# First pair of an FFT-then-SoLU kernel: its loads of x in 128 rows, the small tables elsewhere in the queue, the weight conversions in another order

## The chip, the cores and the metric

The kernel runs on one core of a Trainium2 chip. A core has five engines that run their own instruction streams and wait for each other on semaphores: TensorE (PE, matrix products; PEld is its weight load), VectorE (DVE), ScalarE (ACT), GpSimd (POOL) and SyncE (SP), which only issues transfers. Sixteen DMA engines move the data between the chip's memory (HBM) and the on-chip memory (SBUF, 128 partitions). Transfers issued by SP stand in one queue (q1 in the profile), those issued by POOL in another (q0). The metric is the device time of one execution in microseconds (us), lower is better. A profiled execution also gives a span, from the first to the last instruction, a little less than its time.

## The reference, cut to what matters

A two-dimensional Fourier transform of which the real part is kept, then a token-wise two-layer network with a softmax-weighted activation and a normalization:

```python
batch, seq, dim = (8, 3136, 256)
X = np.fft.fft(x, axis=1)
X = np.fft.fft(X, axis=2)
x = X.real.astype(np.float32).reshape(B * S, D)      # 25088 tokens of 256
h = x @ w_in                                         # w_in: 256 x 1024
h_max = np.max(h, axis=-1, keepdims=True)
e = np.exp(h - h_max)
sm = e / (np.sum(e, axis=-1, keepdims=True) + 1e-09)
solu = h * sm
mu = np.mean(solu, axis=-1, keepdims=True)
var = np.mean((solu - mu) ** 2, axis=-1, keepdims=True)
ln = (solu - mu) / np.sqrt(var + 1e-06) * g_ln       # g_ln: 1024
return (ln @ w_out).astype(np.float32)               # w_out: 1024 x 256
```

x and g_ln are 32-bit floats; w_in and w_out arrive as 64-bit floats, which the kernel itself turns into 32-bit ones ("conversions" below).

## The kernel before

The sequence of 3136 is taken as 49 x 64. The batch of 8 is worked in 4 *pairs* of two samples; a pair has 2 x 49 = 98 rows (`PR`), so a tile of x has 98 partitions. For a pair, x comes in 8 *pieces* c = 0 to 7 (`NC`), each of 4 positions x 256 features: `load` (L118) fetches a tile `xa` through SP and, by a gather with row indices from `idx`, the mirrored positions `xb` through POOL. One such transfer is 98 rows of 4 KB. For the first pair, pieces 2 to 5 stand in borrowed buffers (`room`, two of them, each for two pieces), pieces 0, 1 and later 6, 7 in the two `xa` and `xb` buffers, so that pieces 6 and 7 can only be fetched once pieces 0 and 1 are folded.

Per piece DVE adds the mirror (`add_mirror`, L137) and folds the features (`fold`, L153) into `y` (two buffers); PE applies the first transform (`transform1`, L185: eight matmul records a piece, into four PSUM banks in turn), ACT copies the two results to `z` (L218), and SP writes part of them to DRAM (`keep`, L223). Once all eight pieces are there, `turn` (L225) reads them back in another layout as `g`, `transform2` makes the 256 features of a *unit* (one k1 of a pair, 100 units), and the steady loop over units follows: up-projection (L279), softmax, blocks of transposes, down-projection, store.

Besides the first pair's pieces the opening prepares the weights. w_in is loaded in four raw pieces of 512 KB (L581). Each is converted by DVE and ACT: `exponent_in(i)` is one DVE instruction (L584) and three ACT instructions, the confinement (L608, L610, L612); `narrow_in(i)` is four DVE instructions (L584, L625, L628, L634), of which L628 needs the confined exponents. Then PE multiplies the converted w_in by the feature transform Q (`product_in`, L685), and ACT keeps the product as `Wi` (L689). `mid` (L676) makes a small operand from Q on ACT. w_out comes in two transfers of 1 MB into the buffer of pieces 2 and 3 (L700), is converted in the same manner by `exponent_out` and `narrow_out`, scaled by `g_ln`, and summed by `mean_out` (L730). `scale_out` (L704) scales g_ln. `load_tables` (L662) fetches Q (257 KB) and g_ln; F (`f_tab`, 230 KB) is transform 1's table.

The order of the opening is written out by hand (lines 784 to 861, under `manual_schedule`): each engine runs its instructions in the order in which this program text calls them. That holds for the queues too. The opening's transfers on SP are, in order: idx, w_in pieces 0 and 1, xa 0, F, w_in 2, xa 1, w_in 3, xa 2, xa 3, Q, g_ln, xa 4, xa 5, and then, as buffers come free, xa 6, zd of piece 0, xa 7, a row x0, zd of pieces 1 and 2, w_out, the first table T. A DMA that SP issues may first wait for an earlier one, as eight semaphores are used in turn. POOL issues the gathers of pieces 0 to 7 in order. On DVE the conversions 0 and 1 precede piece 0, exponent 2 comes ahead of piece 0, conversion 2 and exponent 3 ahead of piece 1, conversion 3 ahead of piece 2. The lines that fetch g_ln:

```python
662        def load_tables(self):
663            self.Q = fpool.tile([P, KD, D + 1], FP32, tag="ev", name="Q", bufs=1)
664            nc.sync.dma_start(out=self.Q, in_=q_tab.rearrange("(c p) d -> p c d", p=P))
665            nc.sync.dma_start(out=g_ln, in_=moe_g_ln.rearrange("(c p) -> p c", p=P))
```

g_ln thus arrives as 128 partitions of 8 single numbers.

Of the kernel before, what the change touches and what calls it, by code (L numbers as in the profile page):

```python
# [9 lines left out]
FP32 = mybir.dt.float32  # L10
# [7 lines left out]
P = 128  # L18


N1, N2 = 49, 64
NK = N1 // 2 + 1
NH = N2 // 2
PR = 2 * N1
ZR = 4 * NK
CH = 4
NC = NH // CH
# [11 lines left out]
def shared(b, n):  # L39

    return WHOLE // 2 <= b < n - 1 and all(u % NK for u in (2 * b, 2 * b + 1))
# [3 lines left out]
def kernel(  # L45
# [19 lines left out]
    nc = tc.nc  # L65
    B, S, D = x.shape
    FF = moe_w_in.shape[1]
    KF = FF // P
# [4 lines left out]
    x_g = x.rearrange("b (n1 g l) d -> (b n1 g) (l d)", n1=N1, l=CH)  # L73
    x_pn = x.rearrange("b (n1 n2) d -> (b n1) n2 d", n2=N2)
# [3 lines left out]
    xpool = ctx.enter_context(tc.tile_pool(name="xpool", bufs=2))  # L78
# [6 lines left out]
    fpool = ctx.enter_context(tc.tile_pool(name="fpool", bufs=2))  # L85
# [3 lines left out]
    F = const.tile([PR, 6, ZR], FP32, name="F")  # L89
# [6 lines left out]
    ident = const.tile([P, P], FP32, name="ident")  # L96
    neg_half = const.tile([P, 2], FP32, name="neg_half")
    idx = const.tile([P, NP * (NC + NK)], I32, name="idx")
    w_mid = const.tile([P, FF], FP32, name="w_mid")
    g_ln = const.tile([P, KF], FP32, name="g_ln")  # L100
# [17 lines left out]
    def load(pr, c, room=None):  # L118

        r = slice(pr.p * PR, (pr.p + 1) * PR)  # L120
        if room is None:
            xa = xpool.tile([PR, CH, D], FP32, tag="xa", name="xa")
            xb = xpool.tile([PR, CH, D], FP32, tag="xb", name="xb")
        else:
            xa, xb = (t.rearrange("p (l d) -> p l d", d=D) for t in room)
        nc.sync.dma_start(out=xa, in_=x_pn[r, c * CH + 1 : (c + 1) * CH + 1, :])
        i = pr.p * NC + c
        nc.gpsimd.indirect_dma_start(
            out=xb.rearrange("p l d -> p (l d)"), out_offset=None, in_=x_g,
            in_offset=bass.IndirectOffsetOnAxis(ap=idx[0:PR, i : i + 1], axis=0))  # L130
        x0 = None
        if c == NC - 1:
            x0 = xpool.tile([PR, 1, D], FP32, tag="x0", name="x0", bufs=1)
            nc.sync.dma_start(out=x0, in_=x_pn[r, 0:1, :])
        pr.raw[c] = (xa, xb, x0)

    def add_mirror(pr, c, engine, part=None):  # L137

        xa, xb, _ = pr.raw[c]
        rows = (0, CH) if part is None else (part * CH // 2, (part + 1) * CH // 2)  # L140
        r = slice(rows[0], min(rows[1], CH - 1 if c == NC - 1 else CH))
        a, rb = xa[:, r, :], xb[:, ::-1, :][:, r, :]
        i = engine.tensor_tensor(out=a[:, :, 1:D], in0=a[:, :, 1:D], in1=rb[:, :, D - 1 : 0 : -1], op=ALU.add)
        if part is None:
            engine.tensor_tensor(out=a[:, :, 0:1], in0=a[:, :, 0:1], in1=rb[:, :, 0:1], op=ALU.add)
        return i
# [6 lines left out]
    def fold(pr, c):  # L153

        xa, _, x0 = pr.raw.pop(c)
        pr.y[c] = xpool.tile([PR, CH, D], FP32, tag="y", name="y")
        sides = [(pr.y[c], xa)]
        if c == NC - 1:
            pr.y0 = xpool.tile([PR, 1, D], FP32, tag="y0", name="y0", bufs=1)
            sides.append((pr.y0, x0))  # L160
        for o, i in sides:
            fold_features(o, i)
            nc.vector.tensor_copy(out=o[:, :, 0:129:128], in_=i[:, :, 0:129:128])  # L163
# [473 lines left out]
    class Weights:  # L637
# [24 lines left out]
        def load_tables(self):  # L662
            self.Q = fpool.tile([P, KD, D + 1], FP32, tag="ev", name="Q", bufs=1)
            nc.sync.dma_start(out=self.Q, in_=q_tab.rearrange("(c p) d -> p c d", p=P))
            nc.sync.dma_start(out=g_ln, in_=moe_g_ln.rearrange("(c p) -> p c", p=P))

        def load_table(self, i):
            k1 = slice(KG, NK) if i else slice(0, KG)
# [32 lines left out]
                                  in_=moe_w_out.bitcast(I32).rearrange("(c p) f -> p c f", p=P)[:, c])  # L701

        def scale_out(self):
            nc.scalar.mul(out=g_ln, in_=g_ln, mul=2.0 ** -20)  # L704

        def exponent_out(self, i):
            self.units.append(exponent(moe_w_out, self.raw[:, 2 * i * NW : 2 * (i + 1) * NW]))
# [76 lines left out]
    with tc.manual_schedule():  # L784
        pairs = [Pair(p) for p in range(NP)]
        first, weights = pairs[0], Weights()
# [3 lines left out]
        rooms = {}  # L790
        for c in range(2, 6, 2):
            room = fpool.tile([P, 2, KF, 4, 64], FP32, tag="uT", name="room", bufs=2)
            room = room[0:PR].rearrange("p w c i m -> p (w c i m)").rearrange("p (a n) -> p a n", a=4)
            rooms[c], rooms[c + 1] = [room[:, i] for i in (0, 1)], [room[:, i] for i in (2, 3)]
        weights.load_in()
        for c in range(4):
            weights.piece_in(c)
            if c:
                load(first, c - 1, rooms.get(c - 1))
            if c == 1:  # L800
                nc.sync.dma_start(out=F, in_=f_tab)
        load(first, 3, rooms[3])
        weights.load_tables()
        for c in range(4, 6):
            load(first, c, rooms[c])
        nc.vector.memset(ones, 1.0)
        nc.vector.memset(neg_half, -0.5)
        bits(top_bit, neg_half[:, 0:1].bitcast(I32), 31, ALU.logical_shift_right, 31, ALU.logical_shift_left)
# [6 lines left out]
        for c in range(NC):  # L815

            if c == 0:
                weights.narrow_in(0)
                weights.narrow_in(1)
            elif c < 3:  # L820
                weights.narrow_in(c + 1)
            if c < 2:
                weights.exponent_in(c + 2)
            add_mirror(first, c, nc.vector)
            fold(first, c)
            if c == NC - 1:
                for i in range(2):
                    weights.exponent_out(i)
                confine(weights.units[0], True)
                weights.narrow_out(0)  # L830
            if c + 6 < NC:
                load(first, c + 6)
            if c == 3:
                weights.place_out()
                for i in range(2):
                    weights.load_out(i)
                weights.load_table(0)
                weights.mid()
                weights.scale_out()
            for s in range(CH // 2):  # L840
                if c == NC - 1:
                    confine(weights.units[0], parts=(s,))
                transform1(first, c * CH // 2 + s)
            if c == 3:
                weights.keep_in(0, weights.product_in(0))
            elif c == 4:
                odd = weights.product_in(1, (0,))
            elif c == 5:
                weights.product_in(1, (1,), odd)
# [136 lines left out]
        for i in range(whole + 1, len(units) + lag + 1):  # L986
# [84 lines left out]
            if i in (len(units), len(units) + 1):  # L1071
                w = i - len(units)
# [7 lines left out]
def _tables(B, S, D):  # L1080

    import numpy as np

    def cs(num, den):
        a = 2.0 * math.pi * (num % den) / den
        return np.cos(a), np.sin(a)

    n1, k1 = np.arange(N1)[:, None], np.arange(NK)[None, :]
    c, s = cs(n1 * k1, N1)
    cm, sm = cs((n1 - N1 // 2) * k1, N1)  # L1090
    zero = np.zeros_like(c)
    tabs = [(c, s), (s, -c), (c, zero), (s, zero), (zero, cm), (zero, sm)]
    f = np.zeros((2, N1, 6, NK, 2, 2))
    for t, (u, v) in enumerate(tabs):
        for b in range(2):
            f[b, :, t, :, b, 0], f[b, :, t, :, b, 1] = u, v
    k = (np.arange(NK)[:, None] + N1 * np.arange(N2)[None, :])[None]
    n2 = (np.arange(NH) + 1) % NH
    c, s = cs(n2[:, None, None] * k, S)
    t = np.stack([c, -s])  # L1100
    t[1, -1] = 1.0 - 2.0 * (k[0] % 2)
    m, d = np.arange(D)[:, None], np.arange(D)[None, :]
    q = np.where(d <= D // 2, cs(m * d, D)[0], -cs(m * (d - D // 2), D)[1])

    q = np.concatenate([q, q[:, D // 2 : D // 2 + 1]], axis=1)
    q[:, D // 2] = 0.0
    sign = np.where(np.arange(P) == 0, 1.0, -1.0)[:, None]
    row = np.arange(B)[:, None] * N1 + np.arange(N1)[::-1]

    load = row.reshape(-1, PR, 1) * (N2 // CH) + N2 // CH - 1 - np.arange(NC)  # L1110
    mirror = np.zeros((P, B // 2 * (NC + NK)), np.int32)
    mirror[:PR, : B // 2 * NC] = load.transpose(1, 0, 2).reshape(PR, -1)
    rows = np.arange(B)[:, None, None] * S + (N1 - np.arange(NK)) + N1 * np.arange(N2)[::-1, None]
    rows = rows.reshape(B // 2, P, NK).transpose(1, 0, 2).reshape(P, -1)
    for b in range(rows.shape[1] // 2):
        if shared(b, rows.shape[1] // 2):

            two = rows[:, 2 * b : 2 * b + 2].reshape(2, 2, 32, 2).transpose(1, 0, 3, 2)
            rows[:, 2 * b : 2 * b + 2] = two.reshape(2, P).T
    mirror[:, B // 2 * NC :] = rows  # L1120
    return {
        "f_tab": f.reshape(PR, 6, ZR).astype(np.float32),
        "t_tab": t.reshape(2 * NH, NK, N2).astype(np.float32),
        "q_tab": q.astype(np.float32),
        "sign": sign.astype(np.float32),
        "mirror": mirror,
    }
# [32 lines left out]
```

## Time and profile before

| what | us |
|---|---|
| median of 3 runs (lowest, highest) | 1126.72 (1125.56, 1128.06) |
| the profiled execution | 1127.41 |
| its span | 1125.6 |
| first matmul of piece 0 | 18.80 |
| first matmul of piece 1 | 26.64 |
| first matmul of pieces 2 and 3 | 31.71 |
| first weight product on PE | 37.96 |
| w_out's first conversion on DVE | 47.66 |
| first matmul of transform 2 | 57.36 |

The rows below the span are starts in the timeline of the profiled execution, counted from the span's start. In the profile a line such as `L143` is a line of the kernel's text; a name such as `y<-xa` tells what an instruction writes and reads; `xN` counts instructions that were merged into one row. Idle time in brackets is that of the engine just before the row, with the engine and instruction, or the transfer, that ended it. PE's granted clock over the span is 0.999 of full speed.

### The profile page before, as it was taken

The numbers are of one execution on the slowest core, as the hardware profiler recorded it, in microseconds if no ns is written. First come the engines' busy times: TensorE is split into PE (matmuls) and PEld (weight loads), VectorE is DVE, ScalarE is ACT, GpSimd is POOL, SyncE is SP. The second block draws the span as 40 slices with busy tenths as digits, with TensorE's granted clock in tenths as the row PEclk, the third lists the DMA queues.
The fourth block names the chain that finished last, engine by engine and source line by source line (L and its number), as shares of the span: only waits on it lengthen the run. The fifth ranks groups of instructions, "written<-read, shape, count | busy, mean of one in ns | idle before, by whom it ended". The sixth has DMA issues, their size and how long they took to land. (4 is left out here: it accounts for less than half of the span.)

```text
span 1125.6 us, 22002 instructions
## 1 busy us (share of the span) xinstructions
PE 1093.1 (97%) x7030; PEld 874.1 (78%) x7030; DVE 980.5 (87%) x1440; ACT 798.2 (71%) x1946; POOL 807.5 (72%) x707
## 2 busy tenths in 40 slices
PE   1999999999999999999999999999999999999998
PEld 1556888787787787878877787878877788778888
DVE  6899889888889888898888988898988899888984
ACT  3578777777766777777767777777776777777771
POOL 3048888776887888865878788876776676766665
PEclk9999999999999999999999999999999999999999
DMA  9773798766978889766889797876786785865665
GB/s 236 211 205 82 172 188 202 175 148 152 176 174 167 194 181 187 195 146 144 158 165 183 173 192 181 200 179 143 154 154 143 141 163 125 157 144 112 142 133 126
DMA packets 458569, 185.77 MB, mean 165 GB/s; under 512 B 425774, under 2 KB 440374, under 8 KB 458456
## 3 DMA queue, kind: packets, MB, share of 16 engines
q1 hardware_dynamic: 444568, 145.96, 62.3%
q0 software_dynamic: 13888, 38.42, 13.2%
q8 instruction: 57, 0.93, 0.4%
q14 instruction: 56, 0.46, 0.1%
HBM read 44.78 MB, written 38.80 MB: 74 GB/s over the span
## 5 line engine op out<-in xcount | busy, mean ns | idle before, releaser
L279 PE MATMUL ps_h<-Wi,q 128*128 128x512 f32 x800 | 361.6, 593 | 0.5 <-DVE nmax L300 0.2
L455 POOL TENSOR_TENSOR S<-uT 128x512 f32<-128x512 f32 x186 | 237.3, 1276 | 107.1 <-DVE u L315 35.8
L462 PE MATMUL ps_m<-Ws,S 128*128 128x128 f32 x2304 | 296.0, 275 | 0.0
L462 PEld LDWEIGHTS ps_m<-Ws,S 128*128 128x128 f32 x2304 | 279.5, 192 | 3.2 <-issue 0.2
L322 ACT ACTIVATE h<-u,usum 128x1024 f32<-128x1024 f32 x196 | 225.0, 1148 | 72.3 <-DVE u L315 72.3
L279 PEld LDWEIGHTS ps_h<-Wi,q 128*128 128x128 f32 x800 | 144.2, 190 | 145.0 <-issue 141.9
L315 DVE SCALAR_TENSOR_TENSOR u<-h,u 128x1024 f32<-128x1024 f32 x196 | 233.8, 1228 | 10.9 <-ACT u L308 10.8
L308 ACT ACTIVATE u<-h,nmax 128x1024 f32<-128x1024 f32 x196 | 223.3, 1141 | 2.3 <-DVE nmax L300 1.1
L386 DVE STREAM_TRANSPOSE v<-u 128x2048 f32<-128x2048 f32 x88 | 203.4, 2311 | 3.1
L462 PE MATMUL ps_m<-Wo,uT 128*128 128x128 f32 x1536 | 203.7, 276 | 0.0
L462 PEld LDWEIGHTS ps_m<-Wo,uT 128*128 128x128 f32 x1536 | 187.9, 192 | 1.2 <-issue 1.2
L300 DVE CUSTOM_DVE_ANT_0 h<-ev,ps_h 128x1024 f32<-128x1024 f32 x100 | 122.1, 1221 | 17.1 <-DVE ev L292 9.2
L549 POOL DMA_INDIRECT out_dram<-ot,idx x96 | 111.1, 1157 | 30.0 <-issue 12.8
L300 DVE CUSTOM_DVE_ANT_0 h<-h,ps_h 128x1024 f32<-128x1024 f32 x96 | 117.2, 1221 | 14.6 <-DVE nmax L300 0.7
L455 POOL TENSOR_TENSOR S<-uT,S 128x512 f32<-128x512 f32 x93 | 118.8, 1277 | 7.2
L455 POOL TENSOR_TENSOR S<-S,uT 128x512 f32<-128x512 f32 x93 | 118.6, 1276 | 7.3
L292 DVE SCALAR_TENSOR_TENSOR ev<-w_mid,r,ps_h 128x1024 f32<-128x1024 f32 x99 | 122.8, 1241 | 0.9 <-PE ps_h L279 0.7
L462 PE MATMUL ps_m<-Ws,uT 128*128 128x128 f32 x768 | 101.8, 276 | 0.0
L462 PE MATMUL ps_m<-Wo,S 128*128 128x128 f32 x768 | 101.4, 275 | 0.0
L215 PE MATMUL ps_m<-y,F 98*100 98x258 f32 (+3 forms) x288 | 72.7, 388 | 25.9 <-DVE y L163 24.2
L243 PEld LDWEIGHTS ps_m<-T,g 128*128 128x128 f32 x400 | 60.1, 191 | 47.3 <-issue 45.7
L497 ACT ACTIVATE ot<-ps_m,rs 128x256 f32<-128x256 f32 x96 | 45.4, 473 | 70.4 <-PE ps_m L462 50.4
(109 smaller groups left out, 1232.1 us busy)
## 6 DMA issues: line engine op xcount, KB each, us to landing
uT<-v SPq DMA_DIRECT2D x752, 128.0 KB
g<-zd POOLq DMA_DIRECT2D x72, 160.0 KB, 5.0
out_dram<-ot SPq DMA_DIRECT2D x176, 64.0 KB
xa<-in_x_dram SPq DMA_DIRECT2D x28, 392.0 KB
zd<-z SPq DMA_DIRECT2D x24, 400.0 KB
raw_in<-in_moe_w_in_dram SPq DMA_DIRECT2D x4, 512.0 KB
raw_out<-in_moe_w_out_dram SPq DMA_DIRECT2D x2, 1024.0 KB
room<-in_x_dram SPq DMA_DIRECT2D x4, 392.0 KB
```

Source lines behind the costliest of these rows:

```text
L215: nc.tensor.matmul(o[..., cs], F[:, 2 * t + h, :], i[..., cs], start=first, stop=True, skip_group_check=True)
L243: nc.tensor.matmul(o, g[:, k, h * P : (h + 1) * P], table, start=(h == 0), stop=True, skip_group_check=True)
L279: nc.tensor.matmul(ps[:, fs], t.q[:, c * P : (c + 1) * P], Wi[:, c, fs], start=True, stop=not whole_even)
L292: nc.vector.scalar_tensor_tensor(out=t.ev, in0=w_mid, scalar=t.r, in1=ps, op0=ALU.mult, op1=ALU.add)
L300: nc.vector.tensor_tensor_reduce(out=t.h[s], in0=t.h[0] if s else t.ev, in1=t.odd, scale=1.0 if s else -0.5, scalar=3.0e38, op0=ALU.add, o ...
L308: nc.scalar.activation(out=t.u[s], in_=t.h[s], func=ACT.Exp, bias=t.nmax[:, s : s + 1], scale=-1.0, accum_out=t.esum[:, s : s + 1])
L315: t.last = nc.vector.scalar_tensor_tensor(out=t.u[s], in0=t.h[s], scalar=-1.0, in1=t.u[s], op0=ALU.mult, op1=ALU.mult, accum_out=t.usum[:, ...
L322: nc.scalar.activation(out=t.h[s], in_=t.u[s], func=ACT.Square, bias=t.usum[:, s : s + 1], scale=-float(FF), accum_out=t.ssq[:, s : s + 1])
L386: nc.vector.transpose(out=t.batch.v[:, :, t.w], in_=t.both.rearrange("p s (g n) -> p (s g) n", n=32))
L455: i = engine.tensor_tensor(out=S[j], in0=a, in1=b, op=op)
L462: nc.tensor.matmul(o, a[:, c], b[:, c], start=start and c == 0, stop=c == n - 1, skip_group_check=True)
L549: dma = nc.gpsimd.indirect_dma_start(out=out, out_offset=bass.IndirectOffsetOnAxis(ap=idx[:, i : i + 1], axis=0), in_=t.ot[s], in_offset=None)
```

## The change

- `load` takes 128 rows (`P`) for the first pair, both for `xa` and for the gather of `xb`; the tiles and the borrowed rooms have 128 partitions, and everything that computes reads rows 0 to 97 of them. Rows 98 to 127 are loaded and not read. The index table gets row numbers for those rows. Other pairs load 98 rows as before; the row x0 too.
- g_ln is fetched by `load_gain` as 8 rows of 128 numbers into a buffer of another tile's rotation (`ot1`), and `scale_out` turns it into 128 x 8 by a transpose on PE into a PSUM bank, from which ACT's scaling reads.
- On SP the order becomes: idx, w_in pieces 0 and 1, xa 0, F, g_ln, w_in 2, xa 1, xa 2, w_in 3, xa 3, xa 4, xa 5, Q, and then xa 6 and the rest as before.
- Exponent 2 comes between piece 0's `add_mirror` and `fold` and no longer ahead of both; conversion 2 stays ahead of piece 1; exponent 3 goes from ahead of piece 1 to between piece 2's `add_mirror` and `fold`; conversion 3 goes from ahead of piece 2 to behind its fold. The confinements on ACT move with the exponents: that of exponent 3 now follows the copies of piece 1.
- `mid` goes behind piece 3's transform; `scale_out` stays ahead of it.

```diff
--- before.py
+++ after.py
@@ -118,16 +118,18 @@
     def load(pr, c, room=None):
 
         r = slice(pr.p * PR, (pr.p + 1) * PR)
+        rows = PR if pr.p else P
         if room is None:
-            xa = xpool.tile([PR, CH, D], FP32, tag="xa", name="xa")
-            xb = xpool.tile([PR, CH, D], FP32, tag="xb", name="xb")
+            xa = xpool.tile([P, CH, D], FP32, tag="xa", name="xa")
+            xb = xpool.tile([P, CH, D], FP32, tag="xb", name="xb")
         else:
             xa, xb = (t.rearrange("p (l d) -> p l d", d=D) for t in room)
-        nc.sync.dma_start(out=xa, in_=x_pn[r, c * CH + 1 : (c + 1) * CH + 1, :])
+        nc.sync.dma_start(out=xa[0:rows], in_=x_pn[r.start : r.start + rows, c * CH + 1 : (c + 1) * CH + 1, :])
         i = pr.p * NC + c
         nc.gpsimd.indirect_dma_start(
-            out=xb.rearrange("p l d -> p (l d)"), out_offset=None, in_=x_g,
-            in_offset=bass.IndirectOffsetOnAxis(ap=idx[0:PR, i : i + 1], axis=0))
+            out=xb[0:rows].rearrange("p l d -> p (l d)"), out_offset=None, in_=x_g,
+            in_offset=bass.IndirectOffsetOnAxis(ap=idx[0:rows, i : i + 1], axis=0))
+        xa, xb = xa[0:PR], xb[0:PR]
         x0 = None
         if c == NC - 1:
             x0 = xpool.tile([PR, 1, D], FP32, tag="x0", name="x0", bufs=1)
@@ -662,7 +664,10 @@
         def load_tables(self):
             self.Q = fpool.tile([P, KD, D + 1], FP32, tag="ev", name="Q", bufs=1)
             nc.sync.dma_start(out=self.Q, in_=q_tab.rearrange("(c p) d -> p c d", p=P))
-            nc.sync.dma_start(out=g_ln, in_=moe_g_ln.rearrange("(c p) -> p c", p=P))
+
+        def load_gain(self):
+            self.gain = fpool.tile([P, D], FP32, tag="ot1", name="gain", bufs=3)[0:KF, 0:P]
+            nc.sync.dma_start(out=self.gain, in_=moe_g_ln.rearrange("(c p) -> c p", p=P))
 
         def load_table(self, i):
             k1 = slice(KG, NK) if i else slice(0, KG)
@@ -701,7 +706,9 @@
                                   in_=moe_w_out.bitcast(I32).rearrange("(c p) f -> p c f", p=P)[:, c])
 
         def scale_out(self):
-            nc.scalar.mul(out=g_ln, in_=g_ln, mul=2.0 ** -20)
+            ps = result(2)[:, 0:KF]
+            nc.tensor.matmul(ps, self.gain, ident[0:KF, 0:KF], is_transpose=True, start=True, stop=True)
+            nc.scalar.mul(out=g_ln, in_=ps, mul=2.0 ** -20)
 
         def exponent_out(self, i):
             self.units.append(exponent(moe_w_out, self.raw[:, 2 * i * NW : 2 * (i + 1) * NW]))
@@ -790,19 +797,20 @@
         rooms = {}
         for c in range(2, 6, 2):
             room = fpool.tile([P, 2, KF, 4, 64], FP32, tag="uT", name="room", bufs=2)
-            room = room[0:PR].rearrange("p w c i m -> p (w c i m)").rearrange("p (a n) -> p a n", a=4)
+            room = room.rearrange("p w c i m -> p (w c i m)").rearrange("p (a n) -> p a n", a=4)
             rooms[c], rooms[c + 1] = [room[:, i] for i in (0, 1)], [room[:, i] for i in (2, 3)]
         weights.load_in()
-        for c in range(4):
-            weights.piece_in(c)
-            if c:
-                load(first, c - 1, rooms.get(c - 1))
-            if c == 1:
-                nc.sync.dma_start(out=F, in_=f_tab)
-        load(first, 3, rooms[3])
+        weights.piece_in(0)
+        weights.piece_in(1)
+        load(first, 0)
+        nc.sync.dma_start(out=F, in_=f_tab)
+        weights.load_gain()
+        weights.piece_in(2)
+        for c in range(1, 6):
+            load(first, c, rooms.get(c))
+            if c == 2:
+                weights.piece_in(3)
         weights.load_tables()
-        for c in range(4, 6):
-            load(first, c, rooms[c])
         nc.vector.memset(ones, 1.0)
         nc.vector.memset(neg_half, -0.5)
         bits(top_bit, neg_half[:, 0:1].bitcast(I32), 31, ALU.logical_shift_right, 31, ALU.logical_shift_left)
@@ -817,12 +825,14 @@
             if c == 0:
                 weights.narrow_in(0)
                 weights.narrow_in(1)
-            elif c < 3:
-                weights.narrow_in(c + 1)
-            if c < 2:
-                weights.exponent_in(c + 2)
+            elif c == 1:
+                weights.narrow_in(2)
             add_mirror(first, c, nc.vector)
+            if c in (0, 2):
+                weights.exponent_in(2 + c // 2)
             fold(first, c)
+            if c == 2:
+                weights.narrow_in(3)
             if c == NC - 1:
                 for i in range(2):
                     weights.exponent_out(i)
@@ -835,13 +845,13 @@
                 for i in range(2):
                     weights.load_out(i)
                 weights.load_table(0)
-                weights.mid()
                 weights.scale_out()
             for s in range(CH // 2):
                 if c == NC - 1:
                     confine(weights.units[0], parts=(s,))
                 transform1(first, c * CH // 2 + s)
             if c == 3:
+                weights.mid()
                 weights.keep_in(0, weights.product_in(0))
             elif c == 4:
                 odd = weights.product_in(1, (0,))
@@ -1110,6 +1120,8 @@
     load = row.reshape(-1, PR, 1) * (N2 // CH) + N2 // CH - 1 - np.arange(NC)
     mirror = np.zeros((P, B // 2 * (NC + NK)), np.int32)
     mirror[:PR, : B // 2 * NC] = load.transpose(1, 0, 2).reshape(PR, -1)
+
+    mirror[PR:, :NC] = np.arange(PR, P)[:, None] * (N2 // CH) + N2 // CH - 1 - np.arange(NC)
     rows = np.arange(B)[:, None, None] * S + (N1 - np.arange(NK)) + N1 * np.arange(N2)[::-1, None]
     rows = rows.reshape(B // 2, P, NK).transpose(1, 0, 2).reshape(P, -1)
     for b in range(rows.shape[1] // 2):
```

## The prediction, made before the changed kernel had run

> **What bounds the kernel now.** I read the page first. TensorE (PE) is busy 97% of the span and at nine tenths or more in every slice but the first two and the last, so a change that touches only the loads of the first pair can pay in the opening alone.
>
> ```profile
> PE 1093.1 (97%) x7030; PEld 874.1 (78%) x7030; DVE 980.5 (87%) x1440; ACT 798.2 (71%) x1946; POOL 807.5 (72%) x707
> ...
> PE   1999999999999999999999999999999999999998
> ...
> DMA  9773798766978889766889797876786785865665
> GB/s 236 211 205 82 172 188 202 175 148 152 176 174 167 194 181 187 195 146 144 158 165 183 173 192 181 200 179 143 154 154 143 141 163 125 157 144 112 142 133 126
> ```
>
> Then the stage table in steps of 5 us (columns: stretch, its length, busy us and count for PE, PEld, DVE, ACT, POOL, then PE clock, DMA share, GB/s). The reader is to see DMA engines at a share of about 1 from 5 to 35 us with only 205 to 285 GB/s moved, while the same engines moved 362 GB/s once the 98-row loads were through.
>
> ```profile
> 10.00:15.00 5.00, 0.00 (x0) 0.00 (x0) 2.41 (x5) 0.19 (x1) 0.85 (x1) 1.00 1.03 259
> 25.00:30.00 5.00, 3.36 (x8) 2.15 (x8) 4.93 (x10) 1.74 (x3) 1.18 (x1) 1.00 0.97 205
> 40.00:45.00 5.00, 5.00 (x19) 3.06 (x18) 4.51 (x11) 2.08 (x3) 0.00 (x0) 1.00 0.99 362
> ```
>
> Last the timeline of the first 60 us (start, length, engine, line, operation; in brackets the idle time before it and who ended it).
>
> ```profile
> 8.77 0.39 SPq L665 DMA_DIRECT2D g_ln<-in_moe_g_ln_dram  x1
> ...
> 11.91 16.60 SPq L126 DMA_DIRECT2D room<-in_x_dram  x2
> 15.66 0.43 DVE L584 TENSOR_SCALAR S<-raw_in 128x512 int32<-128x512 int32 x1 [3.18 <-DMA raw_in<-in_moe_w_in_dram]
> ...
> 23.50 0.43 DVE L584 TENSOR_SCALAR S<-raw_in 128x512 int32<-128x512 int32 x1 [2.37 <-DMA raw_in<-in_moe_w_in_dram]
> ...
> 26.64 3.73 PE L215 MATMUL ps_m<-y,F 98*100 98x258 f32 x8 [4.11 <-DVE y L163]
> ...
> 28.70 0.58 ACT L218 COPY z<-ps_m 100x512 f32<-100x512 f32 x1 [2.52 <-PE ps_m L215]
> ...
> 30.41 0.58 ACT L218 COPY z<-ps_m 100x512 f32<-100x512 f32 x1 [1.12 <-PE ps_m L215]
> ...
> 31.71 6.41 PE L215 MATMUL ps_m<-y,F 98*100 98x258 f32 x16 [1.34 <-DVE y L163]
> ...
> 36.37 1.22 DVE L143 TENSOR_TENSOR room<-room 98x1020 f32<-98x1020 f32 x1 [2.21 <-DMA room<-in_x_dram]
> ...
> 37.96 3.60 PE L685 MATMUL wps<-w_in,Q 128*128 128x512 f32 x8
> ...
> 41.39 1.89 PE L215 MATMUL ps_m<-y,F 98*100 98x258 f32 x8
> ```
>
> VectorE (DVE) waits three times for transfers, 3.18 + 2.37 + 2.21 = 7.76 us. From 37.96 us on PE has no gap worth naming: the first weight product, pieces 4 to 7 of the transform, the other products, then the units. So the change is worth what it moves the start of that product (37.96 us), unless a later input becomes late.
>
> [...] the semaphore of a 98-row load shows one early write and 14 later ones, and on a 128-row load queued behind x (Q) two increments come at 17.5 and 18.5 us and the other fourteen only at 29.7 to 34.5 us. [...] 4096-byte packets took a median of 0.16 us at 2 to 6 us, when mostly 128-row pieces moved, but 0.24 to 0.30 us from 8 to 32 us, with 98-row loads on both queues, and 0.19 to 0.22 us at 34 to 40 us with one queue. No run shows 128 rows of x, so this is not proof. [...] Here the clock record begins at 37.27 us, and a piece of transform 1 has 3.73 us of matmuls before it and 1.89 after.
>
> **The change part by part.**
>
> 128 rows. An engine carries 8 packets of each x transfer, not 7. If they take the 0.16 us of other 128-row loads, a transfer costs 1.28 us instead of 7 x 0.25 = 1.75. Bounds for a packet: 0.16 and 0.25 (unchanged); I take 0.16 to 0.18. After raw pieces 0 and 1, x 0 and F, at about 8.6 us as before, an engine has in packets of 4 KB: weight pieces 2 and 3 16; xa 1 to 7 56; Q 4; the mirrored x 64; three zd writes of 240 KB about 11; in all 151, so 24 us, through at 33 us. The gather's 128 rows cost GpSimd little: the 128-row scatter at L549 takes 1157 ns, the 98-row gathers 990 to 1180.
>
> g_ln and Q. The 4-byte loads of g_ln (1024 elements) leave the queue; 327 and 658 packets of queue 1 stand at 28 to 30 and 30 to 32 us. Their issue blocked SP for the 16.60 us above, since piece 4 and 5 of x sat behind it, which was the wait of 2.21. Now g_ln is 8 rows of 512 B, a transpose of 8 columns on PE (0.2 to 0.9 us, in a PE pause), and the same ACT scaling of 0.20 us. Q goes behind x 5; 108 of the packets at 0.16 bring it at about 26 us, and it is needed after 33. Moving `mid` behind the copies of piece 3 takes its 2 x 0.35 us and the wait for Q off those copies.
>
> DVE in the new order. Nothing is added, so old steps give times. Both first conversions end at 12.4, as before. x 0 and its mirror should be there by 11.5, and weight piece 2 by 12.5: it stands behind 8 + 8 packets from 8.6 us, 2.6 us plus lateness of the last engine. Piece 0 with exponent 2 takes 2.53 + 0.4: 15.3. Conversion 2, 2.45: 17.8. Piece 1, 2.53: 20.3; its y is complete at 20.5. Sum of mirror for piece 2, exponent 3, fold: 23.3. Conversion 3 begins, and its third instruction (L628) needs the exponents confined by ACT.
>
> The new wait. In program order ACT now has both copies of piece 1 ahead of this confinement; before it had it ahead of them. Piece 1 on PE starts at 20.6, at the slow clock. In the old trace (26.64, second copy 30.41 + 0.58) its last copy ends 4.35 us after the first matmul: 24.95. Three confinements at 0.75: 27.2. DVE reached L628 at about 24.35, so it stands 2.9 us; behind it wait all of pieces 3 to 7. After 0.78 + 0.61 piece 3 starts at 28.64, and its y is there at about 31.4.
>
> PE then. Pieces 1 and 2 keep it busy without a gap from 20.6 to between 26.0 and 27.5[...], so the clock rises. The pause until 31.47 is 4 to 5 us. [...] Warm, piece 3 takes 1.73 us and the product starts at 33.2. 37.96 - 33.2 = 4.75 us gained. Next are pieces 4 and 5, by DVE at 33.8 and 36.4 while PE wants them at 36.6 and 39.2, so PE stays the bound; pieces 6 and 7 wait, as before, for y buffers that PE frees. The first half of w_out, issued when piece 3's room is free (31.4), with 1 MB at 390 GB/s lands near 35 and is wanted at 47.66 - 4.75 = 42.9. The two zd-to-g turns and the mean product follow PE and shift with it. About 60 us on, nothing has an absolute time, so the shift reaches the end.
>
> Sum against the profiled execution's own 1127.41 us (span 1125.6 and 1.8 around it): 1127.41 - 4.75 = 1122.7. The median of runs, 1126.72, lies 0.7 lower[...], so I don't subtract that 0.7 again.
>
> **The rivals.** (A) The forecast, 1122.7: loads cease to matter, ACT's order and PE's clock take over.
> (B) The wait on ACT does not bite, since piece 1 runs at the fast clock or copies end earlier. Then piece 3 is folded at 28.4, piece 3 on PE ends at 30.5, and the gain is 7.4: 1120.0. For it: all three DVE waits would go. Against it: 3.73 us per piece twice in a row.
> (C) The clock falls in the pause: piece 3 takes 3.73 us, the product starts at 35.2 and loses some 0.7 more: 39.3 in place of 41.39 for piece 4, gain 2.1, 1125.3. A packet of 0.22 us gives about the same: the change would then not do what its rows are for (8 x 0.22 = 7 x 0.25), and only g_ln's removal pays.
> (D) Slower: the 30 unread rows are paid in full because the slow packets came from the two queues' reads of x and not from row counts. The place is the first half of w_out, queued behind the 151 packets: 167 with its own 16. At 0.25 it lands at 8.6 + 41.8 = 50.4 against 47.66 today: 2.7 us late, 1130.1. Break-even is (47.66 - 8.6) / 167 = 0.234 us a packet; A holds up to (42.9 - 8.6) / 167 = 0.205. Against it: 0.16 us where 128-row loads stand alone, 362 GB/s at 40 to 45 us, and 98-row packets alone at 0.19 to 0.22.
>
> **How the numbers follow.** A 0.63, B 0.12, C with the 0.22 packet 0.15, D 0.10. What this measurement can tell from no change is about 0.2%, 2.25 us, so faster means under 1124.5: A and B, and a little of C, 0.77; same: most of C and the mild end of D, 0.14; slower 0.09. The range 1119.8 to 1125.4 holds B's centre and C's, and leaves D and the edge of B out. The likeliest case alone spans 1121.5 to 1124: half a microsecond of lateness in weight piece 2[...].
>
> **What would show it.** Right: x packets near 0.16 us; the three DMA waits of DVE gone or under 0.5 us each; a new idle time of 2 to 3 us on DVE at the L628 of the fourth conversion, ended by ACT; the first product at 33 to 34 us; the rest shifted by one constant. B shows as no such idle time and a product near 31. C shows as 3.7 us for piece 3. D shows as packets over 0.23 us and DVE waiting for raw_out. The forecast is wrong if the gather of 128 rows arrives later than 12.4 us, or if a wait at 60 to 90 us, where the DMA share is 1 again, doesn't shift with the rest.

## The result, and the profile after

| | before | changed |
|---|---|---|
| median of 22 runs, us | 1126.84 | 1125.59 |
| lowest, highest | 1125.52, 1128.23 | 1123.81, 1126.73 |
| the profiled execution | 1127.41 | 1126.52 |
| its span | 1125.6 | 1124.6 |

The ratio is 0.9987, with an interval of 0.9981 to 0.9993. The changed kernel is faster, but by 1.25 us in the medians where 4 were forecast, and by less than the 0.2% from which the prediction speaks of faster. The profiled execution of the changed kernel is one of the slowest of its 22 runs. The stage table of the changed kernel (columns as before: stretch, length, busy us and count for PE, PEld, DVE, ACT, POOL, PE clock, DMA share, GB/s):

```profile
10.00:15.00 5.00, 0.00 (x0) 0.00 (x0) 3.44 (x7) 0.00 (x0) 0.74 (x2) 1.00 1.00 390
15.00:20.00 5.00, 3.56 (x8) 2.15 (x8) 4.93 (x10) 2.75 (x4) 1.38 (x1) 1.00 1.03 415
25.00:30.00 5.00, 2.18 (x10) 1.41 (x8) 2.13 (x4) 3.69 (x7) 0.00 (x0) 0.87 1.03 400
30.00:35.00 5.00, 2.76 (x7) 1.97 (x8) 4.94 (x11) 0.59 (x1) 0.00 (x0) 0.50 0.69 258
35.00:40.00 5.00, 5.00 (x10) 2.36 (x9) 3.45 (x7) 1.18 (x3) 0.00 (x0) 0.61 0.97 355
```

The transfers did what was hoped: 390 to 415 GB/s where 259 and less moved before, at the same DMA share. In the packet records 4096-byte packets take a median of 0.16 us from 10 to 30 us. But the third last column, PE's granted clock, now has 0.87, 0.50 and 0.61, where the old kernel's table had 1.00 (a table also puts 1.00 where the clock's record has no entry yet, in the old kernel up to 37.27 us). The timeline shows what lies around it:

```profile
13.34 1.22 DVE L145 TENSOR_TENSOR xa<-xa,xb 98x1020 f32<-98x1020 f32 x1 [1.52 <-DMA xb<-in_x_dram,idx]
...
21.49 5.54 PE L217 MATMUL ps_m<-y,F 98*100 98x258 f32 x16 [1.31 <-DVE y L165]
...
25.26 0.59 ACT L220 COPY z<-ps_m 100x512 f32<-100x512 f32 x1 [1.12 <-PE ps_m L217]
25.74 0.72 ACT L610 ACTIVATE S<-S,limits 128x512 f32<-128x512 int32 x1
...
28.01 0.75 DVE L630 SCALAR_TENSOR_TENSOR S<-raw_in,top_bit,S 128x512 int32<-128x512 int32 x1 [2.84 <-ACT S L614]
...
32.24 3.71 PE L217 MATMUL ps_m<-y,F 98*100 98x258 f32 x8 [5.06 <-DVE y L165]
...
35.74 5.17 PE L690 MATMUL wps<-w_in,Q 128*128 128x512 f32 x8
...
40.75 1.89 PE L217 MATMUL ps_m<-y,F 98*100 98x258 f32 x8
```

The three waits of DVE for transfers (7.76 us) are gone, but for 1.52 at the first piece. In their place DVE stands 2.84 us at the last conversion of w_in (L630, which is L628 of the old text), because ACT copies piece 1 (25.26) before it confines the exponents (25.74). In the old kernel this confinement came at 23.96, ahead of the copies at 28.70 and 30.41:

```profile
23.96 0.72 ACT L608 ACTIVATE S<-S,limits 128x512 f32<-128x512 int32 x1 [0.80 <-DVE S L584]
```

Piece 3 comes to PE after a pause of 5.06 us and takes 3.71 us, and the first weight product takes 5.17 instead of 3.60. Piece 4 starts at 40.75, before at 41.39: of 7.76 us of waits 0.64 is left. The first matmuls of later units are 0.65 us earlier at 58 us and 0.71 to 0.72 from 168 to 1039 us; nothing there takes or adds anything. The record of PE's granted clock, start, length in us and share (its last entry, which begins behind PE's last work, is left out):

```
before:   37.27 1085.44 1.0
changed:  25.25    3.41 1.0
          28.66   10.24 0.5
          38.90 1085.44 1.0
```

The clock rose 12 us earlier than before and then fell again. This was no chance of the one execution: the mean granted clock of each of the 22 runs of the changed kernel is 0.995 to 0.997, that of the old kernel's profiled execution 0.999.

### The profile page after: what moved, and what is told of

Same layout as the page of the kernel before. It is cut to its first block, busy times and chain, and to the rows that moved or that the text cites. A ratio compares the mean times of both kernels' runs of the same rounds, so it can differ in the third digit from the quotient of the medians.

```text
span 1124.6 us, 22003 instructions
## 1 busy us (share of the span) xinstructions
PE 1093.9 (97%) x7031; PEld 874.4 (78%) x7031; DVE 980.1 (87%) x1440; ACT 798.3 (71%) x1946; POOL 802.6 (71%) x707
## 5 line engine op out<-in xcount | busy, mean ns | idle before, releaser
L551 POOL DMA_INDIRECT out_dram<-ot,idx x96 | 107.5, 1120 | 27.6 <-issue 10.2
```

Source lines behind the costliest of these rows:

```text
L551: dma = nc.gpsimd.indirect_dma_start(out=out, out_offset=bass.IndirectOffsetOnAxis(ap=idx[:, i : i + 1], axis=0), in_=t.ot[s], in_offset=None)
```

## The experiments

Three questions were open: whether ACT's order or the clock or something behind the opening took the gain; what makes the 128-row transfers fast; and what each part is worth alone. "Piece 4" in the table is the start of its first matmul in the profiled execution; from there to the end of the span it is 1083.9 to 1084.5 us in all twelve kernels.

| run | ratio to before, interval | median, us | first product | piece 4 |
|---|---|---|---|---|
| before | | | 37.96 | 41.39 |
| changed | 0.9987, 0.9981 to 0.9993 | 1125.59 | 35.74 | 40.75 |
| e1, confinement earlier | 0.9967, 0.9956 to 0.9978 | 1122.7 | 32.21 | 35.65 |
| e2, ten filling matmuls | 1.0003, 0.9994 to 1.0012 | 1127.32 | 37.72 | 41.15 |
| e3, 98 rows | 1.0014, 1.0006 to 1.0021 | 1128.9 | 40.49 | 45.38 |
| e4, 112 rows | one run | 1131.87 | 39.30 | 45.83 |
| e5, 128 rows alone | 0.9965, 0.9952 to 0.9977 | 1123.36 | 33.24 | 37.88 |
| e6, g_ln and Q alone | 1.0027, 1.0018 to 1.0037 | 1130.12 | 39.17 | 44.16 |
| e7, five filling matmuls | 0.9969, 0.9957 to 0.9981 | 1123.36 | 33.23 | 36.67 |
| e8, e1, weight piece 3 earlier, a warm PE | 0.9943, 0.9929 to 0.9957 | 1120.94 | 31.81 | 35.25 |
| e9, e6 with the turn earlier | 1.0008, 0.9994 to 1.0022 | 1127.52 | 37.81 | 41.34 |
| e10, e8 with the turn earlier | 0.9951, 0.9937 to 0.9964 | 1120.84 | 30.07 | 33.50 |

**e1: ACT's order.**

```diff
-            if c in (0, 2):
-                weights.exponent_in(2 + c // 2)
+            if c in (0, 1):
+                weights.exponent_in(2 + c)
```

> The changed kernel with exponent 3 one piece earlier (between the mirror sum and the fold of piece 1), so that ACT confines it ahead of the copies of piece 1. Theory 1 (ACT's order opens a pause on PE and the pause drops PE's clock): the 2.84 us wait of DVE at the last conversion goes below 0.3, piece 3 starts on PE near 29.4 us instead of 32.24, the pause on PE shrinks from about 5.1 to about 2.4 us. If the clock survives that, the first weight product starts at about 31.2 and takes 3.6, and the kernel is about 6.5 us faster than before (1120.3); if it still drops, the product starts at about 33.1 and takes about 5.2, and the kernel is 3.0 to 3.7 us faster (1123.4). Theory 2 (something behind the opening takes up any shift): as the changed kernel, 1125.6.

The timeline of e1 on PE:

```profile
22.54 7.11 PE L217 MATMUL ps_m<-y,F 98*100 98x258 f32 x16 [3.68 <-DVE y L165]
29.58 0.22 PE L710 MATMUL ps_m<-ident,gain 8*128 8x8 f32 x1
30.40 1.97 PE L217 MATMUL ps_m<-y,F 98*100 98x258 f32 x8 [0.60 <-ACT g_ln L711]
32.21 3.60 PE L690 MATMUL wps<-w_in,Q 128*128 128x512 f32 x8
```

The wait on ACT is gone, and the pause ahead of piece 3 shrinks from 5.06 to 0.60 us; the clock rises at 29.48 us and stays. Piece 4 is 5.7 us earlier than before, and the time falls by 0.33%, or 3.7 us, where 6.5 us with a kept clock or 3 to 3.7 with a dropped one were expected. The profiled execution was the second fastest of seven. The three slowest runs (1123.63 to 1124.31) are the three with a mean clock of 0.997 or 0.998, the other four (1121.68 to 1122.7) have 0.999, which suggests that this order does not keep the clock in every run. A wait came up that the expectation had not, 2.12 us for weight piece 3, which the earlier exponent needs earlier:

```profile
20.78 0.43 DVE L586 TENSOR_SCALAR S<-raw_in 128x512 int32<-128x512 int32 x1 [2.12 <-DMA raw_in<-in_moe_w_in_dram]
```

That the gain goes through to the end refutes the theory of a loss behind the opening.

**e2 and e7: the clock alone.** The order stays, with its wait on ACT; PE gets work whose result nobody reads, ten matmuls in e2 and five in e7.

```diff
                 transform1(first, c * CH // 2 + s)
+            if c == 2:
+                spare = ps_h.tile([P, FF], FP32, tag="h1", name="spare")
+                for _ in range(10):
+                    nc.tensor.matmul(spare[:, 0:HW], ones, weights.w_in[0][:, 0:HW], start=True, stop=True)
```

> The changed kernel with ten more matmuls of 128x512 on PE behind piece 2, whose result nobody reads, to fill the pause; the wait of DVE stays. Theory 1: the clock record shows no drop near 28.7 us, piece 3 takes 1.9 us instead of 3.71, the first product 3.6 instead of 5.17, and the kernel is about 4 us faster than before (1122.8). Theory 2: 1125.6, with the shift lost later. If the filling matmuls run at the slow clock they take up to 8.6 us and piece 3 is late: 1126 or more.

> As e2, with five unread matmuls of 128x512 instead of ten: the ten ran 8.75 us at the full clock, since each is two records of 0.43, and were themselves what made piece 3 late. Five take 4.3 us from about 27 to 31.4. The wait of 2.84 on ACT stays. Theory 1: no drop of the clock, piece 3 at about 32.2 in 1.9 us, first product at 34 in 3.6, piece 4 at 37.5: about 4 us faster than before, 1122.8 to 1123.3. If only the wait on ACT costs time and not the clock: 1125.6.

PE in e2, and then in e7:

```profile
26.74 8.75 PE L856 MATMUL spare<-w_in,ones 128*128 128x512 f32 x20
...
35.91 1.97 PE L217 MATMUL ps_m<-y,F 98*100 98x258 f32 x8 [0.27 <-ACT g_ln L711]
37.72 3.60 PE L690 MATMUL wps<-w_in,Q 128*128 128x512 f32 x8
```

```profile
26.41 4.46 PE L856 MATMUL spare<-w_in,ones 128*128 128x512 f32 x10
30.80 0.22 PE L710 MATMUL ps_m<-ident,gain 8*128 8x8 f32 x1
31.45 1.94 PE L217 MATMUL ps_m<-y,F 98*100 98x258 f32 x8 [0.43 <-DVE y L165]
33.23 3.60 PE L690 MATMUL wps<-w_in,Q 128*128 128x512 f32 x8
```

e2 missed by a wrong size: each matmul is two records of 0.43 us, so the filling took 8.75 us and delayed piece 3 itself, while the clock stayed up. e7 has the right size. DVE still waits 2.83 us for ACT there, yet piece 4 starts 4.1 us earlier than in the changed kernel; 0.8 of them were there at the start of piece 3 already, since x came earlier in this execution, and 3.3 lie between pieces 3 and 4. The time is 0.31% under the kernel before, and the mean clock of all its runs is 0.999 or 1.0. Work that computes nothing made the kernel 2.2 us faster by the medians: the drop of the clock is what took the gain. The wait on ACT matters mostly because it opens the pause, as e1, without that wait, is only 0.7 us below e7 in the medians.

**e3 and e4: rows.** One number each.

```diff
-        rows = PR if pr.p else P
+        rows = PR                       # e3
+        rows = PR if pr.p else 112      # e4
```

> The changed kernel with 98 rows for the first pair as before; g_ln, Q and the new order stay. If the rows carry the early arrival: packets of 4 KB at 0.24 to 0.28 us again, the stream of x through at about 37 us instead of 30, waits of DVE for x or weight pieces of 3 us or more in total, first product no earlier than 36.5 us, time 1126 to 1127.5. If g_ln and the order alone did it: DVE's waits as in the changed kernel and 1125.6.

> The changed kernel with 112 rows for the first pair: 16 engines with 7 rows each[...]. [...] packets of 4 KB at 0.19 to 0.25 us, so later than 128 rows although fewer bytes move. If the number of engines decides: 0.16 us as with 128 rows, and x through earlier by an eighth. The time says little, within 1.5 us of the changed kernel's 1125.6 either way.

e3 puts the slow packets back (medians of 0.24 to 0.34 us in steps of 2 us from 10 to 40 us) and DVE's waits for transfers with them; the largest is

```profile
30.04 0.43 DVE L586 TENSOR_SCALAR S<-raw_in 128x512 int32<-128x512 int32 x1 [4.21 <-DMA raw_in<-in_moe_w_in_dram]
```

since weight piece 3 stands one place further back in the new queue. The clock rises only at 43.42 us. The time, 1128.9, lies 1.4 us above the range expected: with 98 rows the rest of the change costs 0.14%. The stage table of e4:

```profile
10.00:15.00 5.00, 0.00 (x0) 0.00 (x0) 3.31 (x5) 0.00 (x0) 1.52 (x2) 1.00 1.04 257
25.00:30.00 5.00, 2.12 (x6) 1.01 (x5) 2.78 (x7) 2.82 (x5) 0.00 (x0) 1.00 1.06 248
```

112 rows run on 16 engines, 7 rows each (the semaphores of SP's loads show sixteen late increments and no early one), and still move only 257 GB/s or less; packets of 4 KB take 0.24 to 0.29 us while both queues load x. The number of engines is therefore not what matters. 128 rows from the same memory at the same row pitch take 0.16. What makes 128 rows fast is not shown: 8 rows an engine in place of 7 is one candidate, which no run separates from others, and a row range that starts elsewhere was not tried. The one run of e4 took 1131.87, where a time within 1.5 us of 1125.6 was expected. One run is no measured difference, but its trace shows what came late:

```profile
39.30 6.70 PE L690 MATMUL wps<-w_in,Q 128*128 128x512 f32 x8 [1.45 <-DMA Q<-in_q_tab_dram]
```

x has a seventh more bytes than with 98 rows at packet times that did not fall, Q stands behind it in the queue, and the clock rises only at 45.36 us.

**e5 and e6: the parts alone, on the kernel before.** e5 takes from the change the rows in `load`, the unsliced `room` and the index rows; e6 takes `load_gain`, the new `scale_out`, Q behind piece 5 and the later `mid`.

```diff
+        rows = PR if pr.p else P        # e5; xa, xb and idx with 0:rows
...
                 nc.sync.dma_start(out=F, in_=f_tab)
+                weights.load_gain()     # e6; load_tables without g_ln
...
-        weights.load_tables()
         for c in range(4, 6):
             load(first, c, rooms[c])
+        weights.load_tables()
...
-                weights.mid()
                 weights.scale_out()
...
             if c == 3:
+                weights.mid()
```

> The kernel before with 128 rows for the first pair and nothing else. Theory 1: packets of 4 KB at 0.16 us; DVE's waits for weight pieces 2 and 3 (3.18 and 2.37 us before) shrink to under 1 us each. In this old order ACT confines exponent 3 ahead of the copies of piece 1, so there is no wait at the last conversion. g_ln's single numbers still stand in the queue ahead of pieces 4 and 5, but the queue reaches them earlier, so the wait of 2.21 at piece 4 should go too. First product at 31 to 34 us, time 3 to 6 us under before: 1121.5 to 1124. If the rows need g_ln and Q out of the way: a wait at piece 4 of 2 us or more and 1125 to 1126.5.

> The kernel before with only g_ln in 8 rows (turned by PE), Q behind piece 5 of x and the operand from Q made later; 98 rows, old order of the conversions and of x against the weight pieces. The 16.6 us for which SP stood at pieces 4 and 5 goes, and with it the wait of 2.21 at piece 4; the waits for weight pieces 2 and 3 stay. Expected: first product 0 to 2 us earlier, time 1125 to 1127. A rival says that the slow packets only move the wait to pieces 4 to 7: no change or up to 1 us slower.

PE in e5, and then in e6:

```profile
27.15 2.07 PE L217 MATMUL ps_m<-y,F 98*100 98x258 f32 x8 [1.64 <-DVE y L165]
29.75 3.70 PE L217 MATMUL ps_m<-y,F 98*100 98x258 f32 x8 [0.53 <-DVE y L165]
33.24 4.80 PE L687 MATMUL wps<-w_in,Q 128*128 128x512 f32 x8
37.88 1.89 PE L217 MATMUL ps_m<-y,F 98*100 98x258 f32 x8
```

```profile
31.19 3.70 PE L215 MATMUL ps_m<-y,F 98*100 98x258 f32 x8 [1.34 <-DVE y L163]
34.83 0.27 PE L708 MATMUL ps_m<-ident,gain 8*128 8x8 f32 x1
35.65 3.73 PE L215 MATMUL ps_m<-y,F 98*100 98x258 f32 x8 [0.55 <-ACT g_ln L709]
39.17 5.15 PE L688 MATMUL wps<-w_in,Q 128*128 128x512 f32 x8
```

The rows alone bring 0.35%, more than the whole change. In the profiled execution the clock falls there as well (up at 25.42, down at 28.83, up at 35.66), but the old order has no wait on ACT beyond 0.21 us, the pauses are shorter (1.64 us at most), and most runs keep the clock: the mean is 0.997 in two of the six, 0.999 or 1.0 in the other four. DVE has no wait for x in e5; g_ln and Q in the way of pieces 4 and 5 (SP stands 13.67 us at them) cost nothing once the queue is fast. e6 is slower than before by 0.27%, where no change or a small gain was expected. Its transfers do what was expected: the wait at piece 4 is gone. But the turn of g_ln stands between pieces 2 and 3, piece 3 waits 0.55 us for its scaling, the clock rises at 42.29 instead of 37.27, and the product takes 5.15.

**e9: that cause tested.** The turn and the scaling of e6 go behind piece 0.

```diff
-                weights.scale_out()
...
                 transform1(first, c * CH // 2 + s)
+            if c == 0:
+                weights.scale_out()
```

> e6 (g_ln and Q alone) with the turn of g_ln and its scaling behind piece 0 instead of between pieces 2 and 3. Theory: e6 was 3 us slower than before because the turn and the wait of piece 3 for its scaling on ACT (0.55 us) broke the stretch of PE work that raises the clock: it rose at 42.29 us instead of 37.27, and the first product took 5.15 us. With the turn out of the way pieces 2 and 3 follow each other without a gap as before: clock up by 38 us, product at 37 to 38.5 in 3.6 to 4.2 us, 1126 to 1127.5. If the turn is not the cause: 1130.

```profile
31.76 6.22 PE L215 MATMUL ps_m<-y,F 98*100 98x258 f32 x16 [1.18 <-DVE y L163]
37.81 3.69 PE L688 MATMUL wps<-w_in,Q 128*128 128x512 f32 x8
```

PE's timeline in e9: pieces 2 and 3 in one stretch, the clock up at 36.90, and the time as before. Piece 4 is 2.8 us earlier than in e6. About 0.8 of them are the turn and the wait themselves; the rest is the clock. Moving g_ln and Q is then worth nothing at 98 rows.

**e8 and e10: a better version.** e1, with weight piece 3 ahead of x 2 in the queue, and matmuls of ones that keep PE busy; e10 has the turn of g_ln behind piece 0 as well.

```diff
-            if c == 2:
+            if c == 1:
                 weights.piece_in(3)
...
+        def keep_warm(n):
+            for _ in range(n):
+                nc.tensor.matmul(spare[:, 0:P], ones, ones, start=True, stop=True)
...
+        keep_warm(50)
...
                 transform1(first, c * CH // 2 + s)
+            keep_warm({0: 14, 1: 3, 2: 14}.get(c, 0))
```

> e1 (exponent 3 one piece earlier) with weight piece 3 loaded ahead of x 2 instead of behind it, and unread 128x128 matmuls of ones on PE before piece 0 (50) and behind pieces 0, 1 and 2 (14, 3, 14), so that the clock is up before the first piece. Theory 1: DVE's wait for weight piece 3 (2.12 us in e1) goes below 0.3, pieces 0 to 3 take 1.9 us each, first product at about 30.5 us or earlier: 7 us faster than before, 1119.5 to 1121, and less spread from run to run. If the added matmuls stand in the way of pieces: as e1, 1122.7, or slower.

> e8 (exponent 3 and weight piece 3 earlier, PE kept busy) with the turn of g_ln behind piece 0. The gap of 0.27 us ahead of piece 3 that ACT's scaling ends goes; the clock is up anyway, so no more than that: 0 to 0.5 us faster than e8's 1120.94.

In e10's timeline on PE

```profile
28.29 1.94 PE L217 MATMUL ps_m<-y,F 98*100 98x258 f32 x8
30.07 3.60 PE L690 MATMUL wps<-w_in,Q 128*128 128x512 f32 x8
33.50 1.89 PE L217 MATMUL ps_m<-y,F 98*100 98x258 f32 x8
```

piece 4 is at 33.50, 7.9 us ahead of the kernel before; over the runs the ratio is 0.9951, about 5.5 us. In e8 the wait for weight piece 3 is gone as expected, but the first product comes at 31.81 where 30.5 was expected; the time is in the range expected. e8 (five runs, 1120.29 to 1121.23) and e10 (1119.6 to 1121.38) can't be told apart by their times and both beat the changed kernel by more than 4 us; how much of this each of the added edits brings was not separated. A spread of about 1 to 2 us in place of 3 goes with a mean clock of 0.999 or 1.0 in all ten runs, but that was not tested by itself, and five runs are few.

## Where the prediction held and where it failed

- **What bounds the kernel: right.** A shift of piece 4 goes through to the end in every run, within 0.6 us.
- **128 rows: right.** Packets of 0.16 us, the last piece of x landed by 32.8 us against 33 forecast. Rival D, with its packet of 0.25, fell with it; e4, with 16 engines and packets of 0.24 to 0.29, shows that it is not the number of engines that makes the difference. Why 128 rows are fast stays open.
- **g_ln and Q: what went was worth less.** SP's 16.6 us and the wait of 2.21 went as said, but e5 shows that with fast packets that wait goes by itself, and e6 and e9 that alone it brings nothing.
- **DVE's steps: nearly right.** Conversion 1 ended at 11.8 rather than 12.4, but the first gather was complete at 13.3, not by 11.5: eleven engines had finished their share by 11.0, five between 11.8 and 13.3. That is later than the 12.4 which the prediction names as a sign of being wrong, and it cost 0.77 us at piece 3. But it belongs to this execution: in those of e1, e2 and e7, with the same loads up to there, the first gather was whole at 11.6 to 12.0 and DVE did not wait for it. Piece 3 came to PE at 32.24 instead of 31.47.
- **The new wait on ACT: right**, 2.84 us against 2.9, at the instruction and for the reason named.
- **PE then: the step that failed.** It takes piece 3 as warm after a pause of 4 to 5 us. In the old kernel's trace no pause at the full clock is longer than 0.7 us, so that the clock would outlast this one was the author's estimate. The profiled execution had the drop of rival C: piece 3 took 3.50 us to the start of the product where 1.73 stands in the sum, and the product 5.01 where 3.43 stands. That is 3.35 us, and with the 0.77 of the late first gather it makes 4.1, the distance between 36.6 and 40.75. The clock had stood at 1.0 for 3.41 us when it fell at 28.66; PE had worked until 27.0 (27.2 with the turn of g_ln), so it fell 1.5 us into the pause. In e5 it had stood at 1.0 for 3.41 us too when it fell at 28.83, 1.7 us after a pause of 1.64 was over. In e8 a pause of 1.45 us, ahead of piece 0, did no harm: piece 0 took 1.97 us, where it takes 3.73 at the slow clock. Nor was the drop rare: by the mean clock, 0.995 to 0.997, it is there in all 22 runs. For this step rival C had it right. e7 shows the size: the same kernel with a kept clock, 1123.36, near the forecast of 1122.7.
- **The number.** 1125.59 lies at the upper edge of the range that was given, and near the 1125.3 of rival C, which is in part luck. C names the drop, but has piece 4 at 39.3, where it came at 40.75, and takes a gain of 2.1 us off an execution of the old kernel that is slower than its median; 1.25 us were measured.
- The sign was given by the rows, as argued. Rival B's early end of ACT's copies did not occur; what e1 did by another order, a first product at 32.2, lies between A and B.

## What to carry to other kernels

Before an opening is reordered, look for the engine whose in-order queue joins two chains: here ACT's copies of one piece stood ahead of a conversion that all of w_in waited for, and DVE stood 2.84 us. A gain on transfers can be lost to PE's clock when it pulls PE's first pieces apart, here by 5.06 us, with the clock at 0.5 for 10.24 us; bunch the early matmuls, or fill the pauses with unread ones (e7, 2.2 us faster by the medians), and measure the fillers' length in the trace first. Loading 30 rows that nobody reads, 1125.59 us, was cheaper than loading 98, e3's 1128.9.

## What the runs showed of the hardware that was not expected

- Where PE's clock fell, it had been at 1.0 for 3.41 us, both in the changed kernel and in e5, and it stayed at 0.5 for 10.24 us in the one and 6.83 in the other, three times and twice that. From the start of a stretch that PE filled to the rise of the clock it took 3.76 us (from 21.49) and 6.66 (from 32.24) in the changed kernel, 5.56 before (from 31.71), 5.14 in e9 (from 31.76) and 6.94 in e1 (from 22.54). What sets the time within this range stays open.
- 112 rows on 16 engines moved x at 237 to 257 GB/s from 10 to 35 us, 128 rows at 390 to 415 from 10 to 30: the fewer bytes came later.
- In the profiled execution of the changed kernel the gathers of the first pair completed in two groups, eleven engines together and five up to 2.3 us behind, at every piece from 0 to 6. In e1, e2, e5 and e7, with 128 rows too, the first gather shows no such group; its sixteen engines finish within 1.2 to 1.8 us of each other, where they took 3.0. The cause stays open.
